# Linear attention in a four-layer kernel: denominators moved from TensorE matmuls to row sums on GpSimd and VectorE, with the order of keys, values and queries changed

## The chip, the cores and the metric

The kernel runs on one core of a Trainium2 chip. The metric is the device time of one execution in microseconds (us), as a median of several runs. The profile is one execution taken by the hardware profiler; its span is 1.75 to 2.93 us shorter than the time that is quoted for a run.

## The reference, cut to what matters

Four layers over 2048 tokens of width 1024: linear attention, feed-forward, linear attention, feed-forward, each with a layer norm in front and a residual sum behind. Only the attention layers are touched:

```
phi = lambda t: where(t > 0, t + 1, exp(t)) + 1e-6
pq, pk = phi(q), phi(k)                       # 32 heads of 32
kv  = einsum("bhsd,bhse->bhde", pk, v)
z   = pk summed over the tokens               # [head, d]
num = einsum("bhqd,bhde->bhqe", pq, kv)
den = einsum("bhqd,bhd->bhq", pq, z) + 1e-6   # one number per token and head
o   = (num / den) @ wo
```

Both kernels fold the output weight into kv (T = kv @ wo, once per layer), so the output is (pq / den) @ T.

## The kernel before

Queries are made feature-major (features in the partitions, 512 tokens in the columns). The sum z falls out of the key-value matmuls through a column of ones beside the values. The denominator is a matmul with z spread over each head's block; its reciprocal is exp(-ln(den)) on ScalarE.

```
def phi(self, ps, out):
    e = self.ep.tile([P, NW], F32, tag="e")
    nc.scalar.activation(out=e, in_=ps, func=ACT.Exp)
    nc.vector.tensor_scalar(out=e, in0=e, scalar1=1.0, scalar2=1e-6, op0=ALU.min, op1=ALU.add)
    nc.vector.scalar_tensor_tensor(out=out, in0=ps, scalar=0.0, in1=e, op0=ALU.max, op1=ALU.add)
...
def den(sc, g):                                # 32 per layer: 4 token groups x 8 feature tiles
    p = pq[sc, g // 4][:, g % 4, :]
    ps = self.ps3.tile([P, NW], F32, tag="b")
    nc.tensor.matmul(ps, lhsT=zrep[:, g, :], rhs=p, start=True, stop=True)
    r = self.ep.tile([P, NW], F32, tag="e")
    nc.scalar.activation(out=r, in_=ps, func=ACT.Ln, bias=self.eps6[:, 0:1])
    nc.scalar.activation(out=r, in_=r, func=ACT.Exp, scale=-1.0)
    nc.vector.tensor_tensor(out=p, in0=p, in1=r, op=ALU.mult)
...
later.at(4, finish_kv)
q_units(0, 5); fold_wo()                       # all 16 fold matmuls in one go
q_units(1, 2); out_units(0)
q_units(2, 2); out_units(1)                    # each q unit later makes one den
q_units(3, 2); out_units(2); out_units(3)
```

## Time and profile before

| | before |
|---|---|
| time, median | 1668.13 us |
| span in the profile | 1665.9 us |
| TensorE busy | 99% of the span |
| VectorE, ScalarE, GpSimd busy | 34%, 22%, 0% |
| denominator matmuls | 64 |

How to read it: a 512-column matmul has a record of 379 ns, but its successor starts after 216 ns. Busy time therefore says little. Time between two starts beyond the usual 216 ns is called a hole here; an eviction is the copy of a matmul's result out of PSUM, where this kernel's matmuls write. The lines that show the pace and the holes stand in the prediction.

### The profile page before, as it was taken

To read this page: it belongs to the slowest core of one execution; us is meant where nothing else is said; L and a number is where in the kernel's file an instruction comes from. 1 tells how busy PE (TensorE), PEld (TensorE's weight loads), DVE (VectorE), ACT (ScalarE), POOL (GpSimd) and SP (SyncE) were. 2 spreads that over 40 slices of the span, in tenths; PEclk is the share of its full clock that TensorE was granted. 3 is DMA by queue.
4 is the path that set the end of the run, shared out by engine and by line. 5 is a ranking of instruction groups with operands and counts; after the bars stand their busy time and mean duration, and the time that the engine had idled before them with its cause. 6 is when DMAs were issued, how large, how long until landed. Compare 5 with 4: busy or idle time off the path is not lost.

```text
span 1665.9 us, 18656 instructions
## 1 busy us (share of the span) xinstructions
PE 1644.1 (99%) x7678; PEld 751.3 (45%) x7834; DVE 571.6 (34%) x975; ACT 364.9 (22%) x695; POOL 4.8 (0%) x38
## 2 busy tenths in 40 slices
PE   8999999999999999999999999999999999999999
PEld 4444444444444444444444444444444444444444
DVE  7338994113221311311142398922111111111111
ACT  4337541100110110011033374411001101101110
POOL 0000000000000000000000000000000000000000
PEclk9999999999999999999999999999999999999999
DMA  9322134446445645644520312344554464455440
GB/s 297 57 64 89 32 95 127 142 145 171 153 138 186 177 142 158 170 154 138 174 75 1 94 58 45 95 121 144 186 169 149 142 190 147 144 178 164 149 153 28
DMA packets 262006, 218.28 MB, mean 131 GB/s; under 512 B 67232, under 2 KB 260000, under 8 KB 261920
## 3 DMA queue, kind: packets, MB, share of 16 engines
q1 hardware_dynamic: 257312, 212.88, 42.8%
q10 hardware_dynamic: 4608, 4.20, 0.7%
q8 instruction: 61, 1.00, 0.2%
q14 instruction: 25, 0.20, 0.0%
HBM read 197.13 MB, written 4.19 MB: 121 GB/s over the span
## 4 chain that ended last, share of the span: by engine, by line
PE 92%; DVE 4%; ACT 2%; issue 1%; DMA 1%; SPq 0%; another core or an unknown queue 0%
PE pg L433 23%; PE acc L450 23%; PE pu L433 23%; PE ps L295 13%; PE ps L364 4%; PE ps L377 4%; DVE stats L133 1%; PE kv L266 1%; DVE xn L149 1%; DVE x L384 1%; PE ps L335 1%; ACT r L337 1%; DMA x<-in_A_x_dram 1%; DVE pq L339 0%; ACT r L338 0%
## 5 line engine op out<-in xcount | busy, mean ns | idle before, releaser
L433 PEld LDWEIGHTS <-t 128*128 128x128 bf16 x3584 | 350.7, 98 | 422.9
L433 PE MATMUL pg<-xnT,t 128*128 128x512 bf16 x1757 | 420.2, 379 | 1.9
L433 PE MATMUL pu<-xnT,t 128*128 128x512 bf16 x1755 | 419.9, 379 | 1.9
L450 PE MATMUL acc<-t,hT 128*128 128x512 bf16 x1756 | 386.2, 379 | 1.9
L439 DVE TENSOR_TENSOR hT<-pu,rg 128x512 bf16<-128x512 f32 x224 | 154.9, 691 | 591.1 <-PE pu L433 568.7
L438 ACT ACTIVATE rg<-pg 128x512 f32<-128x512 f32 x224 | 133.6, 597 | 764.9 <-PE pg L433 690.3
L450 PEld LDWEIGHTS <-hT 128*128 128x128 bf16 x1792 | 175.4, 98 | 211.4
L295 PE MATMUL ps<-t,xnT 128*128 128x512 bf16 x999 | 224.3, 379 | 2.3 <-DVE xnT L201 0.8
L295 PEld LDWEIGHTS <-xnT 128*128 128x128 bf16 x1024 | 98.8, 98 | 115.3 <-DVE xnT L201 1.2
L364 PE MATMUL ps<-xnT,t 128*128 128x512 bf16 x500 | 119.8, 379 | 0.7
L377 PE MATMUL ps<-T,pq 128*128 128x512 bf16 x501 | 111.7, 379 | 0.6
L238 DVE TENSOR_SCALAR e<-e 128x512 f32<-128x512 f32 x128 | 54.3, 424 | 129.9 <-ACT e L237 129.0
L237 ACT ACTIVATE e<-ps 128x512 f32<-128x512 f32 x128 | 76.4, 597 | 91.5 <-PE ps L295 69.9
L140 ACT ACTIVATE rstd<-mv,eps 128x1 f32<-128x1 f32 x64 | 18.7, 294 | 306.9 <-DVE mv L138 306.6
L133 DVE BATCH_NORM_STATS2 stats<-x 128x6 f32<-128x512 f32 (+1 forms) x120 | 81.5, 685 | 2.0
L461 DVE TENSOR_TENSOR xo<-x,acc 128x512 bf16<-128x512 f32 x32 | 22.0, 688 | 171.8 <-PE acc L450 169.9
L377 PEld LDWEIGHTS <-pq 128*128 128x128 bf16 x512 | 50.1, 98 | 59.0
L364 PEld LDWEIGHTS <-t 128*128 128x128 bf16 x512 | 49.7, 98 | 55.0 <-issue 1.0
L458 DVE TENSOR_TENSOR x<-x,acc 128x512 f32<-128x512 f32 x32 | 21.6, 676 | 149.6 <-PE acc L450 148.4
L149 DVE TENSOR_SCALAR xn<-x,mv,rstd 128x1024 bf16<-128x1024 f32 (+2 forms) x65 | 47.8, 737 | 25.5 <-DMA xnT<-xn 18.3
L301 ACT ACTIVATE pkv<-ps 128x512 bf16<-128x512 f32 x64 | 38.1, 599 | 66.2 <-PE ps L295 64.4
L339 DVE TENSOR_TENSOR pq<-pq,r 128x512 bf16<-128x512 bf16 x64 | 43.6, 689 | 7.7 <-ACT r L338 5.6
(42 smaller groups left out, 377.8 us busy)
## 6 DMA issues: line engine op xcount, KB each, us to landing
t<-in_B_W_gate_dram SPq DMA_DIRECT2D x56, 1024.0 KB, 5.8
t<-in_B_W_up_dram SPq DMA_DIRECT2D x56, 1024.0 KB, 5.3
t<-in_B_W_down_dram SPq DMA_DIRECT2D x64, 896.0 KB, 5.7
t<-in_A_wqkv_dram SPq DMA_DIRECT2D x11, 1024.0 KB, 5.6
t<-in_A_wo_dram SPq DMA_DIRECT2D x4, 1024.0 KB, 5.3
out_dram<-xo ACTq DMA_DIRECT2D x32, 128.0 KB, 2.4
x<-in_A_x_dram SPq DMA_DIRECT2D x15, 256.0 KB, 7.8
t<-in_A_wqkv_dram SPq DMA_DIRECT2D x2, 512.0 KB, 5.1
```

The costliest lines, as they stand in the source:

```text
L133: self.nc.vector.bn_stats(out=stats[:, c, :], in_=src[:, c * fmax:(c + 1) * fmax])
L149: self.nc.vector.tensor_scalar(out=xn[:, s], in0=src[:, s], scalar1=mv[:, 0:1], scalar2=rstd[:, 0:1], op0=ALU.subtract, op1=ALU.mult)
L237: nc.scalar.activation(out=e, in_=ps, func=ACT.Exp)
L238: nc.vector.tensor_scalar(out=e, in0=e, scalar1=1.0, scalar2=1e-6, op0=ALU.min, op1=ALU.add)
L295: nc.tensor.matmul(ps, lhsT=self.xnT[l, q][:, kt, j * P:(j + 1) * P], rhs=w[:, kt, :], start=(kt == 0), stop=(kt == KT - 1))
L339: nc.vector.tensor_tensor(out=p, in0=p, in1=r, op=ALU.mult)
L364: nc.tensor.matmul(ps, lhsT=w[:, kt, (g % 4) * P:(g % 4 + 1) * P], rhs=self.xnT[l, sc][:, kt, :], start=(kt == 0), stop=(kt == KT - 1))
L377: nc.tensor.matmul(ps, lhsT=pq[sc, g // 4][:, g % 4, j * P:(j + 1) * P], rhs=T[g // 2][:, g % 2, n2 * NW:(n2 + 1) * NW], start=(g == 0), s ...
L433: nc.tensor.matmul(ps, lhsT=w[:, kt, fi * P:(fi + 1) * P], rhs=self.xnT[l, q][:, kt, :], start=(kt == 0), stop=(kt == KT - 1))
L438: nc.scalar.activation(out=rg, in_=pg, func=ACT.Relu)
L439: nc.vector.tensor_tensor(out=h[:, fi, :], in0=pu, in1=rg, op=ALU.mult)
L450: nc.tensor.matmul(acc[j], lhsT=hT[ft // 4][:, ft % 4, j * P:(j + 1) * P], rhs=wd[:, k, :], start=(ft == 0), stop=(ft == self.FT - 1))
```

## The change

The intent is to take the denominators off TensorE. Queries become token-major (128 tokens in the partitions), so that a denominator is the sum of 32 neighbouring columns of pq times z. GpSimd adds up the key features (`k_sum`), multiplies by z (`z_mult`) and scales (`z_scale`); VectorE sums rows and takes the reciprocal. The scaled queries are then transposed by DMA to serve as stationary operands (the ones that a weight load brings in: 512 loads of pqT in the changed kernel). So that GpSimd has time for it, all keys come before the values of the last two token groups, and queries alternate with these values, with the fold, and with the first outputs. Most of the query's phi moves from VectorE to ScalarE (three activations; one VectorE op stays). The weight ring shrinks from 7 tiles to 5, and two PSUM pools from 3 + 1 to 2 + 2.

The core of the diff, cut (the head's loads, pools and lists of units are left out):

```
-        def den(sc, g):
-            ... matmul with zrep, Ln, Exp(-), multiply ...
+        def k_sum(t):
+            if t == 0:
+                nc.gpsimd.tensor_copy(out=ksum, in_=pk[t])
+            else:
+                nc.gpsimd.tensor_tensor(out=ksum, in0=ksum, in1=pk[t], op=ALU.add)
+        def z_row():                           # round, sum over partitions and broadcast
+            nc.scalar.activation(out=hi, in_=ksum, func=ACT.Copy)
+            for i in range(H):
+                nc.tensor.matmul(ps, lhsT=self.ones, rhs=hi[:, i * NW:(i + 1) * NW], ...)
+                nc.scalar.activation(out=zrow[:, i * NW:(i + 1) * NW], in_=ps, func=ACT.Copy)
+        def q_unit(sc, j, c, lag):
+            nc.scalar.activation(out=e, in_=ps, func=ACT.Relu, scale=-1.0)
+            nc.scalar.activation(out=e, in_=e, func=ACT.Exp, scale=-1.0)
+            nc.scalar.activation(out=e, in_=e, func=ACT.Identity, bias=self.eps6[:, 0:1])
+            nc.vector.scalar_tensor_tensor(out=pq[...], in0=ps, scalar=0.0, in1=e, max, add)
+        def z_mult(pq, sc, j):
+            nc.gpsimd.tensor_tensor(out=prod, in0=pq, in1=zrow, op=ALU.mult)
+        def z_sum(pq, prod, sc, j):
+            nc.vector.tensor_reduce(out=den, in_=heads(prod), axis=X, op=ALU.add)
+            nc.vector.tensor_scalar(out=den, in0=den, scalar1=1e-6, scalar2=None, op0=ALU.add)
+            nc.vector.reciprocal(out=den, in_=den)
+        def z_scale(pq, den, sc, j):
+            nc.gpsimd.tensor_tensor(out=heads(pq), in0=heads(pq), in1=den broadcast, op=ALU.mult)
+            nc.sync.dma_start_transpose(out=pqT[sc][:, :, j * P:(j + 1) * P], in_=pq)
...
+        # values and keys of groups 0 and 1, keys of 2 and 3, then:
+            later.at(4, z_row)
+            run(q_of(0, 4), v_then_kv(2))
+            run(q_of(1, 1), v_then_kv(3))
+            later.at(2, finish_kv)
+            run(q2[:5])
+            run([with_fold(u, i) for i, u in enumerate(q2[5:] + q3[:5])])   # 2 folds per unit
+            run(q3[5:], out0[:3])
```

## The prediction

The sum came to 1643.5 + 2 x (0.3 + 1 + 2 + 1) = 1652 us. Of its terms, the 0.3 (key blocks) and the first 1 (broadcast of the key sums) stand as guesses of mine, worked out from no trace. So do the 1660 to 1668 of the last rival. The floor and the 2 and 1 us at the fold come from the trace of the kernel before, with the choices that the text names. Its "about 0.73 with bias" is an estimate that fits that trace: 0.636 us for an activation without bias (L338) plus the 0.690 - 0.597 between L337 with one and L237 without. The one pace is seen in the chain of waits, where 49 matmuls take 10.74 us on L295, L377 and L450 alike.

> **What bounds the kernel now.** I read the page's busy line first, then the chain of waits, then the groups of instructions with their shapes kept apart, then the timeline of TensorE where the chain leaves it.
>
> ```profile
> PE 1644.1 (99%) x7678; PEld 751.3 (45%) x7834; DVE 571.6 (34%) x975; ACT 364.9 (22%) x695; POOL 4.8 (0%) x38
> PE 92%; DVE 4%; ACT 2%; issue 1%; DMA 1%; SPq 0%; another core or an unknown queue 0%
> ```
>
> TensorE is busy 99% of the span and is 92% of the chain that ended last; no other engine passes 34%. The kernel is a matmul stream with small holes. The real pace is read from the chain in order of time, near its end:
>
> ```profile
> 1618.94 10.74 PE acc L450 x49
> 1629.73 10.74 PE acc L450 x49
> 1640.52 10.74 PE acc L450 x49
> ```
>
> The pieces start 10.79 us apart. Each shows 49 matmuls of a period of 50 (a record goes missing now and then, which the count of weight loads confirms: 1792 loads against 1756 matmuls on that line). So one 512-column matmul costs 10.79/50 = **0.2158 us**, although its record says 379 ns[...]. The pace is one constant for all stages.
>
> I add up by weight loads: the feed-forward layers have 3584 + 1792 = 5376, which is 1160.2 us. The attention layers have 1024 (keys and values) + 512 (queries) + 512 (outputs) = 2048, which is 442.0 us; 64 denominators, 13.8 us; 32 for folding the output weight, 6.9 us. The 256 key-value products start 8 in 0.48 us (40.35 to 40.83 in the timeline), 0.06 each, 15.4 us. Sum 1638.3 of a span of 1665.9. The other 27.6 us: by 19.59 us only 33 projections (7.1 us) had been started, so the head costs 12.5; the last matmul ends at 1662.5, so the tail costs 3.4. The remaining **11.7 us** are holes, and some small transposes, inside the attention layers. The timeline and the waits of TensorE show the holes:
>
> ```profile
> 145.52 3.57 PE L349 MATMUL ps<-t,kvT 128*128 128x512 bf16 x12
> 149.29 0.38 PE L349 MATMUL ps<-t,kvT 128*128 128x512 bf16 x1 [0.20 <-ACT T L352]
> ...
> 181.47 4.48 PE L364 MATMUL ps<-xnT,t 128*128 128x512 bf16 x20
> 186.76 0.39 PE L335 MATMUL ps<-pq,zrep 128*128 128x512 bf16 x1 [0.82 <-DVE pq L239]
> ```
>
> Denominator matmuls (L335) stop the stream until VectorE has made the query features; the fold (L349) runs ahead of its evictions: 12 matmuls take 3.57 us where the pace gives 2.6.
>
> [...]
>
> **The change part by part.** The groups it removes are these:
>
> ```profile
> L335 PE MATMUL ps<-pq,zrep 128*128 128x512 bf16 x64 | 23.9, 384 | 4.2 <-DVE pq L239 3.9
> L337 ACT ACTIVATE r<-ps,eps 128x512 f32<-128x512 f32 x64 | 43.4, 690 | 9.5 <-PE ps L335 9.2
> L338 ACT ACTIVATE r<-r 128x512 f32<-128x512 f32 x64 | 39.9, 636 | 1.5
> L339 DVE TENSOR_TENSOR pq<-pq,r 128x512 bf16<-128x512 bf16 x64 | 43.6, 689 | 7.7 <-ACT r L338 5.6
> ```
>
> Only the first lies on the path: 64 x 0.2158 = 13.8 us, not the 23.9 of its busy time. Added on TensorE are 4 matmuls that broadcast the key sums (0.9 us); the 16 small transposes of the key-value matrix become a DMA transpose. If every hole also closed, the gain would be 13.8 + 11.7 - 0.9 = **24.6 us**: a floor of 1668.1 - 24.6 = 1643.5. Nothing else shortens the stream: projections, outputs, fold and feed-forward keep their counts, head and tail their order. A gain over 2% needs 1634.8, out of reach by this sum.
>
> What comes back, per attention layer:
> - Keys. GpSimd adds 16 key tiles[...] in bursts of four (one per 1.73 us unit, in the second half of each block)[...]. I put 0.3 us.
> - Key sums. [...] ScalarE rounds it (kvT's 1024 columns took 1.02 us). The broadcast stands in TensorE's order after four units, 6.9 us. TensorE waits some 1 us.
> - Queries beside values. Per token tile TensorE has 6.9 us. ScalarE: two queries of three activations (0.60 + 0.64 + about 0.73 with bias) and two values (0.60), 5.1[...]. No loss.
> - Fold among queries. The build order puts the first fold after five query units: 5 x 1.73 + 0.5 = 9.1 us. Its input needs the last key-value product (2.2 us), the masking behind the second query's eviction on VectorE (about 7.9), then a DMA transpose; the layer-norm ones landed in a median 3.1 us, up to 9.9 behind weights. So 11 to 13 us: a wait of 2 us or a bit more. From there a unit is 1.73 + 2 x 0.216 = 2.16 us for TensorE, against ScalarE 1.97 + 0.60 = 2.57[...]. Eight units: ScalarE falls 3.3 us behind; buffers and the wait just paid hide most. I put 1 us.
> Sum 0.3 + 1 + 2 + 1 = 4.3 us, twice 8.6. **1643.5 + 8.6 = 1652 us.** Where I chose: the lag that buffers hide (I let them hide two thirds) and the 2 us wait.
>
> The weight ring shrinks from 7 to 5 tiles. In the feed-forward a pair is used in 32 matmuls x 2 = 13.8 us and loaded in 5.8 + 5.3 us; the second of a pair is issued at the start of the pair before and needed 15.5 us later. It fits, so I give it nothing.
>
> **The rivals.**
> - GpSimd becomes the bound. If an op on bf16 with a broadcast operand took 4 us, the 16 last query ops in the pure-query stretch (8 tiles x 8 us = 64 against 40) would stop the stream some 20 us per layer, since VectorE's reduction waits in order for the product and there is one product buffer. Time about 1690 to 1705.[...]
> - The ring starves the feed-forward. If each of 56 pairs waited 0.5 us, +28: 1680. For it: the DMA share is 0.5 there, and transposes share the queue; against: 11.1 of 15.5 us.
> - All hidden: the buffers absorb everything, 1644.
> - The gain vanishes[...]: 1660 to 1668.
>
> **Range and chances.** The low end is the floor, 1643.5, rounded to 1643. The high end, 1664, takes about 10 us back per layer. Faster by over 2% contradicts the matmul count: 0.02. Slower by over 2% (1701) needs slow GpSimd ops or a starving ring: 0.04. Within 2%: 0.94.
>
> **What would show it.** Right: no denominator matmuls, weight loads down by 76 (64 + 16 removed, 4 added), the same 0.2158 pace, feed-forward stages of the same length to 1 us[...], and TensorE's waits at the fold on the DMA of kvT and at the key-sum broadcast on ScalarE. Wrong: GpSimd rows over 3 us, TensorE waiting on evictions all through the key blocks, or weight loads that TensorE waits for in the feed-forward.

## The result

The changed kernel takes **1648.28 us** (1647.47 to 1649.50, 4 runs), against 1667.81 us for the kernel before in the same rounds: 19.5 us less. The ratio is 0.9884, with an interval from 0.9866 to 0.9901. A ratio is the mean time of one kernel's runs over that of the other's of the same rounds, so it is not quite the ratio of the medians.

The busy line, the chain by engine, and three groups of the changed kernel:

```profile
PE 1634.7 (99%) x7758; PEld 747.5 (45%) x7758; DVE 575.1 (35%) x930; ACT 372.2 (23%) x699; POOL 196.5 (12%) x102
...
PE 91%; DVE 3%; ACT 2%; POOL 1%; issue 0%; DMA 0%; DVEq 0%; POOLq 0%
...
L356 POOL TENSOR_TENSOR prod<-pq,zrow 128x1024 f32<-128x1024 bf16 x32 | 68.1, 2128 | 53.4 <-DVE den L361 35.5
...
L299 POOL TENSOR_TENSOR ksum<-ksum,pkv 128x1024 f32<-128x1024 f32 x30 | 65.5, 2182 | 68.9 <-DVE pkv L245 67.7
...
L367 POOL TENSOR_TENSOR pq<-pq,den 128x1024 bf16<-128x1024 bf16 x32 | 61.2, 1911 | 17.9 <-issue 10.6
```

The stream still bounds the kernel; weight loads fell from 7834 to 7758, and GpSimd went from nothing to 196.5 us. What TensorE itself waited for, from the waits of TensorE in the changed kernel (total us, times, longest; the wait before the warm-up is left out):

```profile
PE tp L203 <- DVE xn L152: 2.1, 1, 2.1
PE ps L322 <- ACT hi L319: 1.5, 2, 0.7
PE ps L284 <- DMA t<-in_A_wqkv_dram: 0.9, 1, 0.9
PE ps L284 <- DVE xnT L206: 0.8, 2, 0.5
PE ps L377 <- DMA kvT<-kvm: 0.6, 2, 0.3
PE kv L311 <- DVE pkv L245: 0.6, 1, 0.6
```

The second line is the broadcast of the key sums, the fifth the fold's wait for the transposed key-value matrix, the last a key-value product in the first layer. The others are in the head. Such a wait counts from the modelled end of the matmul before, so it is shorter than the real hole. The real hole is the time between two matmul starts less the usual 0.216 us: 0.9 us per layer at the broadcast (1.121 between starts), 0.51 and 0.44 at the first fold, 0.73 at the key-value product.

With the time of each matmul counted from its start to the next one's start, the trace gives a full account (a missing record's time falls to the matmul before it):

| TensorE, us | before | after |
|---|---|---|
| warm-up and transposes in the head | 7.7 | 6.8 |
| projections of keys, values, queries | 339.5 | 341.0 |
| key-value products | 16.0 | 15.0 |
| transposes of the key-value matrix | 0.9 | 0 |
| denominators, or broadcast of z | 15.5 | 0.9 |
| fold | 9.8 | 7.1 |
| outputs | 110.7 | 110.5 |
| feed-forward layers | 1160.1 | 1160.1 |
| sum | 1660.2 | 1641.4 |

The difference is 18.8 us; the two spans differ by 18.7. The feed-forward is the same to a tenth of a microsecond, so the shorter ring and the smaller PSUM pool cost nothing there. The projections took 331.5 us at the pace in both kernels, so their holes are 8.0 us before and 9.5 after. The row of the key-value products needs care: four missing records of projections put 0.86 us into the 16.0, and the 15.0 contains the hole of 0.73. The runs without denominators below have neither; there they take 15.1 and 14.3 us (59 ns from start to start with 129 columns, 56 with 128). Of the 9.5 us of holes, 4.6 are in the head of this one execution (2.8 before), a matter that the second profile of the same kernel below sets apart.

### The profile page after: what moved, and what is told of

Its sections match the earlier page's. It is cut to its first block, busy times and chain, and to the rows that moved or that the text cites. A ratio compares the mean times of both kernels' runs of the same rounds, so it can differ in the third digit from the quotient of the medians.

```text
span 1647.2 us, 18687 instructions
## 1 busy us (share of the span) xinstructions
PE 1634.7 (99%) x7758; PEld 747.5 (45%) x7758; DVE 575.1 (35%) x930; ACT 372.2 (23%) x699; POOL 196.5 (12%) x102
## 4 chain that ended last, share of the span: by engine, by line
PE 91%; DVE 3%; ACT 2%; POOL 1%; issue 0%; DMA 0%; DVEq 0%; POOLq 0%
PE acc L523 23%; PE pu L506 23%; PE pg L506 23%; PE ps L284 13%; PE ps L389 7%; POOL ksum L299 1%; DVE e L244 1%; PE kv L311 1%; DVE pkv L245 1%; ACT e L347 0%; ACT e L346 0%; ACT T L381 0%; ACT e L348 0%; DVE pq L349 0%; DVE den L361 0%
## 5 line engine op out<-in xcount | busy, mean ns | idle before, releaser
L506 PEld LDWEIGHTS <-t 128*128 128x128 bf16 x3584 | 350.7, 98 | 422.8
L284 PE MATMUL ps<-t,xnT 128*128 128x512 bf16 x1536 | 344.7, 380 | 1.7 <-DMA t<-in_A_wqkv_dram 0.9
L284 PEld LDWEIGHTS <-xnT 128*128 128x128 bf16 x1536 | 149.0, 98 | 177.7 <-issue 5.6
L389 PE MATMUL ps<-T,pqT 128*128 128x512 bf16 x512 | 111.5, 379 | 0.0
L143 ACT ACTIVATE rstd<-mv,eps 128x1 f32<-128x1 f32 x64 | 18.8, 294 | 335.4 <-DVE mv L141 335.4
L389 PEld LDWEIGHTS <-pqT 128*128 128x128 bf16 x512 | 50.1, 98 | 60.4
L356 POOL TENSOR_TENSOR prod<-pq,zrow 128x1024 f32<-128x1024 bf16 x32 | 68.1, 2128 | 53.4 <-DVE den L361 35.5
L299 POOL TENSOR_TENSOR ksum<-ksum,pkv 128x1024 f32<-128x1024 f32 x30 | 65.5, 2182 | 68.9 <-DVE pkv L245 67.7
L349 DVE SCALAR_TENSOR_TENSOR pq<-ps,e 128x512 bf16<-128x512 f32 x64 | 43.4, 679 | 82.0 <-ACT e L348 81.7
L244 DVE TENSOR_SCALAR e<-e 128x512 f32<-128x512 f32 x64 | 52.7, 823 | 48.9 <-ACT e L243 48.5
L367 POOL TENSOR_TENSOR pq<-pq,den 128x1024 bf16<-128x1024 bf16 x32 | 61.2, 1911 | 17.9 <-issue 10.6
L243 ACT ACTIVATE e<-ps 128x512 f32<-128x512 f32 x64 | 38.1, 596 | 70.9 <-PE ps L284 69.6
```

The source lines that it names most:

```text
L284: nc.tensor.matmul(ps, lhsT=self.xnT[l, l_q][:, kt, j * P:(j + 1) * P], rhs=w[:, kt, :], start=(kt == 0), stop=(kt == KT - 1))
L299: nc.gpsimd.tensor_tensor(out=ksum, in0=ksum, in1=pk[t], op=ALU.add)
L349: nc.vector.scalar_tensor_tensor(out=pq[:, c * NW:(c + 1) * NW], in0=ps, scalar=0.0, in1=e, op0=ALU.max, op1=ALU.add)
L356: nc.gpsimd.tensor_tensor(out=prod, in0=pq, in1=zrow, op=ALU.mult)
L367: nc.gpsimd.tensor_tensor(out=heads(pq), in0=heads(pq), in1=den[:, :].unsqueeze(2).to_broadcast([P, D // HD, HD]), op=ALU.mult)
L389: nc.tensor.matmul(ps, lhsT=pqT[sc][:, g, j * P:(j + 1) * P], rhs=T[g // 2][:, g % 2, n2 * NW:(n2 + 1) * NW], start=(g == 0), stop=(g == G ...
```

## The experiments

**1. Where the gain comes from: both kernels without denominators.** The rival to my account was that the new order made the gain. Both runs give wrong results on purpose.

Before without denominators:

```
-                later.at(lag, lambda g=g: den(sc, g))
```

> Before with its denominators left out (wrong result on purpose; their matmuls, activations and multiplications go, everything else stays). Theory: the matmuls (64 x 0.2158 = 13.8 us) and the holes at them (about 6.8 us in the gaps between matmul starts) are the gain, so 1667.8 - 20.6 = 1647, perhaps 1 less since the fold's evictions meet an idler ScalarE. Rival: the gain of the change came from the new order of the parts; then this run stays over 1653.

Measured: **1644.96 us** (1644.16 to 1646.24); before 1667.88. That is 22.9 us less, 2.3 us more than the 20.6 of the theory. Most of the difference is the fold, whose 32 matmuls fell from 9.8 to 8.2 us now that no ln and exp stand among its evictions.

The change without denominators (key sums, broadcast, product, row sum, reciprocal and scaling left out, the DMA transposes kept):

```
-                later.at(1, lambda: k_sum(t))
-            later.at(4, z_row)
-                later.at(lag, lambda: z_mult(pq, sc, j))
+                later.at(lag + 4, lambda: z_scale(pq, None, sc, j))     # only the transpose is left
```

> The changed kernel with its denominators left out (wrong result on purpose: no key sums, no broadcast, no product, row sum, reciprocal or scaling). Theory: what denominators still cost there is the broadcast (4 matmuls, 0.9 us), the wait in front of it (0.9 us per layer) and the hole in the first key block (0.6 us), so 1648.3 - 3.3 = 1645.0; the fold's holes stay, since ScalarE makes them. Rival: GpSimd and VectorE work makes the fold's holes too; then 1643 or less. Against the run of before without denominators: if both are within 3 us of each other, the order of the parts alone is worth little.

Measured: **1645.47 us** (1644.87 to 1646.04). Both kernels without denominators are within 0.5 us, so the rest of the change, the order included, is worth nothing on balance. The denominators cost 22.9 us in the old form and 2.8 us in the new one; the difference is the gain. The rival has fallen. The balance hides two sides, though: the trace of this run saves the transposes of the key-value matrix (0.9 us) and 0.8 us of key-value products, and pays 4.1 us of holes at the fold, where the kernel before without denominators has 1.3 us of holes in its attention layers. With no product, row sum or scaling left, these holes cannot come from them.

**2. What the new form still costs: collisions between VectorE and GpSimd.** In the key blocks the min-and-add of phi is the same instruction in both kernels. First line: the kernel before (all uses of phi), from its source view, with durations min/median/max in ns; second fence: the changed kernel (keys only).

```profile
L238 DVE TENSOR_SCALAR e<-e x128: 408/427/428, 29.1 to 1054.8; 128x512 f32<-128x512 f32 x128
```

```profile
L244 DVE TENSOR_SCALAR e<-e x64: 375/427/2359, 31.1 to 916.3; 128x512 f32<-128x512 f32 x64
```

The median stays at 427 ns, but the maximum goes from 428 to 2359, and the mean to 823 (its group's 52.7 us over 64). The trace shows it one by one: 22 of the 64 records are longer than 0.6 us, and 21 of these start during a key sum on GpSimd and end 0.28 to 0.29 us after that sum. Such an op is called blocked here; the blocked time stands inside its own record. The chain of waits of the changed kernel at the end of the keys, in order of time (start, length), shows what it leads to:

```profile
88.00 1.56 DVE e L244
...
90.27 1.55 DVE e L244
...
98.42 2.18 POOL ksum L299
...
105.22 2.13 POOL ksum L299
...
107.37 1.06 ACT hi L319
...
108.48 0.59 PE ps L322 x2
```

An op that takes 0.42 us when free takes 1.5 to 2 us here, VectorE falls behind, the last four key sums run back to back from 98.42 to 107.35, and the rounded sums reach TensorE 0.9 us late. But is it the collision, or merely GpSimd's own 2.2 us per tile? To take the collision away, phi of the keys was made without the min-and-add ("that op" in the expectation):

```
-            self.phi(project(f"k{c}", q, j), pk[t][:, c * NW:(c + 1) * NW])
+            ps = project(f"k{c}", q, j)
+            e = self.ep.tile([P, NW], F32, tag="e")
+            nc.scalar.activation(out=e, in_=ps, func=ACT.Relu, scale=-1.0)
+            nc.scalar.activation(out=e, in_=e, func=ACT.Exp, scale=-1.0)
+            nc.vector.scalar_tensor_tensor(out=pk[t][...], in0=ps, scalar=1e-6, in1=e, max, add)
```

> The changed kernel with phi of the keys made by two activations (relu of -x, exp of the negative) and one VectorE op[...]; the result stays right. Theory (collisions of that op with GpSimd delay the key sums): GpSimd's last burst ends in time, the wait before the broadcast (0.9 us per layer) and the hole of 0.6 us in the first key block go, 1648.3 - 2.4 = 1646. Rival: GpSimd's own 2.2 us per tile delays it; then the wait stays and the time is 1648.

Measured: **1646.40 us** (1645.59 to 1647.78), correct. The wait for the rounded sums is no longer among TensorE's waits (the hole is 0.15 us), nor is the one of the key-value product. The last four sums still take 8.8 us (8.9 in the changed kernel), but they start 2.85 us before the first query matmul, not 2.25, and are ready 5.9 us after it, not 6.7. These 0.76 us are what the wait lost. So GpSimd's own speed makes most of the delay, and the collisions make the part that TensorE waited for. The edit also takes VectorE's own work away (64 x 0.427 = 27.3 us, beside the 25.4 us of blocked time), and this run cannot part the two; but 0.43 and 0.69 us of work per unit of 1.73 us would not put VectorE behind.

The hole at the first layer's key-value product had another source. The op in front of the late key is a layer-norm scaling (L152) that starts during a key sum and is recorded with 2.35 us, against a median of 0.81. From the chain of the changed kernel:

```profile
43.92 2.27 DVE xn L152
46.19 0.61 DVE pkv L245
46.80 0.05 issue
46.85 0.40 PE kv L311 x4
```

It is still blocked in this run (2.11 us), where the hole is gone, and in the combined version of section 5 the hole is back (0.58 us). So that this edit closed it is not shown.

The same wait can be avoided by order alone:

```
-            later.at(4, z_row)
+            later.at(6, z_row)
```

> The changed kernel with the broadcast of the key sums two units (3.45 us) later in TensorE's order, nothing else. Theory: TensorE's wait of 0.9 us per layer for the rounded key sums was a matter of order alone, and GpSimd, which idles before its first product anyway, does not mind: 1648.3 - 1.8 = 1646.5. Rival: a later start of the products pushes GpSimd's work into the stretch around the fold and gives the gain back there: 1648.

Measured: **1646.34 us** (1646.22 to 1646.71). The hole at the broadcast is 0.24 us per layer, the waits at the fold are as they were, so the products did not push GpSimd's work into the fold. Its theory holds.

**3. The holes at the fold: ScalarE or VectorE.** Windows of the changed kernel around the fold (start:end, length, then busy us of PE, weight loads, VectorE, ScalarE, GpSimd with the number of instructions, then granted clock, DMA share and GB/s):

```profile
160.00:194.00 34.00, 33.39 (x158) 14.79 (x157) 25.98 (x44) 30.65 (x53) 26.62 (x14) 1.00 0.53 124
```

ScalarE has 30.65 of 34 us, the most beside TensorE. The gaps between matmul starts at the fold, beyond the first, are 1.1 us in the first attention layer and 1.2 in the third layer. The third activation of a query only adds 1e-6; it can go into the max:

```
-            nc.scalar.activation(out=e, in_=e, func=ACT.Identity, bias=self.eps6[:, 0:1])
-            nc.vector.scalar_tensor_tensor(out=pq[...], in0=ps, scalar=0.0, ...
+            nc.vector.scalar_tensor_tensor(out=pq[...], in0=ps, scalar=1e-6, ...
```

> The changed kernel with two activations per query unit in place of three (the 1e-6 goes into the max of the VectorE op, a difference far under bf16). Theory: ScalarE, busy 30.65 of 34 us around the fold, makes the holes at the fold (about 1.1 us per layer beyond the wait for the DMA transpose); they go, 1648.3 - 2.2 = 1646. Rival: VectorE's row sums and evictions make them; then under 0.5 us is gained.

Measured: **1645.29 us** (1645.01 to 1646.79), correct: 3.0 us less, not the 2.2 expected, and far over the rival's 0.5. By the trace the holes at the fold fell from 3.25 to 0.58 us, both layers together. The same window in this run:

```profile
160.00:194.00 34.00, 34.00 (x164) 15.51 (x163) 27.60 (x48) 23.00 (x39) 28.02 (x15) 1.00 0.59 143
```

ScalarE is down to 23.00, and TensorE shows no idle time in the window. The wait for the transposed matrix went too, although its DMA takes about as long (3.0 us after 3.1): it was issued 7.4 us after the queries' start, not 8.1, since the masking in front of it stands behind a query's eviction on VectorE, and that waits for ScalarE.

Next, that wait attacked by order: the fold one query unit later.

```
-            run(q2[:5])
-            run([with_fold(u, i) for i, u in enumerate(q2[5:] + q3[:5])])
-            run(q3[5:], out0[:3])
-            run(out0[3:])
+            run(q2[:6])
+            run([with_fold(u, i) for i, u in enumerate(q2[6:] + q3[:6])])
+            run(q3[6:], out0[:2])
+            run(out0[2:])
```

> The changed kernel with the fold starting one query unit (1.73 us) later, beside six units of the last query tile group instead of five. Theory: the wait for the DMA transpose (0.5 us per layer) goes and ScalarE's lag meets the same evictions one unit later, so the other fold holes stay: 1648.3 - 0.95 = 1647.3. Rival: with the wait gone ScalarE has that much less time to catch up, and the fold's holes grow by the same amount: 1648.3.

Measured: **1649.46 us** (1649.01 to 1650.59): worse by 1.2 in the median. The runs overlap with those of the change (up to 1649.50), but the trace has 0.9 us more of holes at the fold. The DMA wait did go, but TensorE's waits now have this:

```profile
PE ps L377 <- DVE T L383: 1.7, 2, 0.8
```

A fold matmul waits for an eviction that now stands behind a row sum on VectorE (1.0 us between starts beyond the pace, in both layers), and ScalarE's holes are still there. My theory fell, and it went even further than the rival: not only is nothing gained, a new wait came.

**4. How much room GpSimd has.** Each product is done twice:

```
             nc.gpsimd.tensor_tensor(out=prod, in0=pq, in1=zrow, op=ALU.mult)
+            nc.gpsimd.tensor_tensor(out=prod, in0=pq, in1=zrow, op=ALU.mult)
```

> The changed kernel with each GpSimd product of query features and key sums done twice (same result). Theory: GpSimd is near its limit around the fold, busy 26.6 of 34 us; 7 more products of 2.13 us there are 41.5 of 34, and VectorE's row sums wait in order for them, so TensorE loses 5 to 8 us per layer: 1658 to 1664. Rival: buffers hide GpSimd's lag; then under 1652. GpSimd busy should read 196.5 + 68 = 265 us.

Measured: **1684.06 us** (1683.69 to 1684.85), slower than before (ratio 1.0098). GpSimd reads 263.9 us busy, as expected; TensorE lost 35.8 us, 17.9 per layer, where I had 5 to 8. From the waits of this run, all engines:

```profile
DVE den L362 <- POOL prod L357: 68.2, 24, 5.2
...
PE ps L378 <- DVE T L384: 10.7, 7, 2.6
PE ps L390 <- DVE x L397: 10.6, 6, 2.5
...
PE ps L284 <- DVE pq L349: 6.0, 3, 2.9
```

VectorE's row sums waited 68.2 us for products (3.9 in the changed kernel), and everything behind them in VectorE's order waited too: fold evictions, query evictions, and the residual sums of the outputs. I had counted the loss only up to the end of the fold and had forgotten that the lag is carried into the outputs: 6.6 us of holes per layer are there. Up to the end of the fold the loss is still some 11 us per layer, so the 5 to 8 were too few there too. The direction is shown: one more 2.13 us op per token tile is more than the schedule holds.

**5. A version that beats both.** First all helpful edits and the later fold together (broadcast one unit later, at 5):

> The version that should beat both: keys' phi with two activations and one VectorE op, two activations per query, the broadcast one unit later, the fold one unit later. Theory: the gains of the single edits add, since each takes away another hole: broadcast 1.8, first key block 0.6, fold 2.2, wait for the transposed key-value matrix 0.95: 1648.3 - 5.6 = 1642.7, within 1 us of the floor of 1643.5 that was computed before. Rival: the holes hide behind each other, so the sum is no more than the best single edit, 1645.

Measured: **1644.22 us** (1644.15 to 1644.78), correct, 1.5 over the theory: the sum of the single gains was not reached. Its waits have a fold eviction on VectorE again (`PE ps L381 <- DVE T L387`, 0.8 us in all), which fits the loss in the run with the later fold alone; the hole at the first key-value product is there too. So the fold went back:

> The version with all three edits that helped (keys' phi with two activations and one VectorE op, two activations per query, broadcast one unit later) but the fold where the change has it. Theory: what held the version with the fold one unit later at 1644.2 was that its fold's eviction stood behind a row sum on VectorE (holes of 0.58 us per layer); with the fold back they go: 1644.2 - 1.2 = 1643.0. Rival: with the earlier fold the wait for the transposed key-value matrix comes back; then 1644 or more.

Measured: **1643.71 us** (1642.54 to 1644.52), correct, ratio to before 0.9852 (0.9836 to 0.9869). The waits of TensorE have no line of the attention layers any more. Its four runs overlap those of the version before it, so the last 0.5 us are shown by the profile, not by the times: the holes at the fold fell from 1.3 to 0.6 us, both layers together. Another 0.5 us between the two profiles is the hole at the first key-value product, which no edit between them touches. The holes in the attention layers add up to about 0.8 us in the trace.

> The changed kernel as it is, on the same chip as the best version. Theory: 1648.3 again, 5 us above the best version; TensorE waits for the rounded key sums in both layers. The half-rate matmuls in the head may or may not come, since only some profiles have them.

Measured: **1648.06 us** (1647.89 to 1649.18), 4.4 above the best version on the same chip. The span of this profile is 1645.7 us, 1.5 less than the first one's, with the same holes in the attention layers to 0.2 us each; the difference is the head. There the first profile has a gap of 2.07 us and behind it six matmuls at 427 ns from start to start, twice the usual. This one has none. So 1.5 us of the first profile's 9.5 us of holes are not the change's.

## Why the prediction was right

The prediction said 1652 (1643 to 1664), within 2%; measured were 1648.28 and 1648.06. It was right, and mostly for its reasons.

- **The bound and the pace.** Right. Weight loads fell by 76, the feed-forward stayed, and the account by starts adds up to the difference of the spans. One reading is rough: 12 fold matmuls up to the end of the last record are 11 x 0.2158 + 0.379 = 2.75 us at the pace, not 2.6.
- **The gross gain of 24.6 us.** Right within the noise. The floor of 1643.5 is what the best version reached (1643.71). Leaving out the denominators gave 22.9, and 1.3 us of holes were left in that run, 1.0 of them before fold matmuls. The only term that was missing is the key-value products, 0.8 us cheaper with 128 columns than with 129.
- **GpSimd's cost.** Measured were 2.18, 2.13 and 1.91 us (key sums in a burst start 2.25 to 2.28 us apart), 196.5 us in all.
- **Given back: 8.6 us predicted; the holes measured in the first profile add up to 5.8.** Term by term, for both layers together:

| hole | predicted | measured |
|---|---|---|
| key blocks | 0.6 | 0.7, in one layer |
| broadcast of the key sums | 2 | 1.8 |
| wait for the transposed matrix | 4 | 0.95 |
| other holes at the fold | 2 | 2.3 |

The term that was off is the wait for the transposed matrix, "2 us or a bit more" per layer, and the step of it that failed is "the build order puts the first fold after five query units: 5 x 1.73 + 0.5 = 9.1 us". The first fold stands behind a sixth unit, which is in the same list item as the fold itself, so it is due after 6 x 1.73 + 0.45 = 10.8 us. The timeline of TensorE in the changed kernel shows it (start, length, instruction):

```profile
158.66 3.62 PE L284 MATMUL ps<-t,xnT 128*128 128x512 bf16 x16
162.11 0.61 PE L311 MATMUL kv<-pkv 128*128 128x128 bf16 x8
162.56 8.80 PE L284 MATMUL ps<-t,xnT 128*128 128x512 bf16 x40
171.70 0.60 PE L377 MATMUL ps<-t,kvT 128*128 128x512 bf16 x2 [0.35 <-DMA kvT<-kvm]
```

The first line is the last value unit and the first unit of the queries, which therefore starts at 162.11 - 1.73 = 160.4; the third line is five more query units. The other times of that step were right: the masking ended and the DMA was issued at 168.54, 8.1 us after the queries' start (7.9 predicted), and took 3.12 us, so the matrix was there after 11.3 (11 to 13 predicted). Against 10.8 that leaves the measured half microsecond. The sum 1643.5 - 0.8 + 5.8 = 1648.5 comes near the measured 1648.28.

- **Cause of the fold's holes.** I put them on ScalarE; the run with two activations shows it.
- **Cause of the broadcast's wait.** Collisions, but not as I had them, and the right 1 us is partly luck: I had put the collisions into the length of the burst of sums, a guess. The burst started 2.25 us before the keys end and lasted 8.9, so ready after 6.7. VectorE's op was blocked (1.5 to 2 us) and GpSimd's sums in the burst were not stretched (2.13 to 2.21 us): the collisions delayed the start.
- **Key blocks.** The number was a guess and is right by luck. Not every min-and-add collided with a key sum (21 of 64), and the one hole stands behind the blocked layer-norm op, which the prediction did not have.
- **The rivals.** The starving ring did not happen: no wait for weights in the feed-forward. "All hidden" did not happen either, but the best version comes near it. GpSimd as the bound did not happen, yet it is close: the run with double products is what that rival described.

What stays open: why the head's wait for a first weight tile is 0.9 us in one profile and absent in others of the same load order.

## What to carry to other kernels

Count the matmuls of a stream that bounds a kernel at their start-to-start pace (0.216 us here, beside a record of 379 ns). Here work taken off the stream was worth that pace and the waits in front of it (22.9 us measured, 20.6 by that count), and the order alone was worth nothing on balance (1644.96 and 1645.47 us without denominators). Work given to GpSimd was cheap here, 2.8 us for all denominators, but two things took time from the stream: key sums that blocked VectorE's ops, in front of the 0.9 us per layer at the broadcast (0.15 in the run without the min-and-add), and row sums that waited in VectorE's order for GpSimd's products, behind the 35.8 us of the run with double products. The first is seen in the maximum (2359 ns), not the median (427), of a VectorE group, the second in VectorE's waits (68.2 us against 3.9). Where a wait remains, look which engine is fullest in that window: taking one activation from ScalarE there, 30.65 of 34 us busy, cut the holes at the fold from 3.25 to 0.58 us, and moving the fold in the order made a new one of 1.0 us per layer. Moving the broadcast did help: its hole fell from 0.9 to 0.24 us per layer.

## Further figures from the traces

- The time for which a key sum on GpSimd blocks a VectorE op stands inside the blocked op's record: 2359 ns at most for the min-and-add, against a median of 427.
- For 1024 columns GpSimd took 2.13 us for bf16 times bf16 to fp32, 2.18 for fp32 plus bf16, 1.91 for bf16 times a broadcast fp32 operand to bf16, and 1.14 for a cast, all in the changed kernel.
- In the head of the changed kernel a gap of 2.07 us (matmul starts 2.45 us apart), with smaller ones in the microseconds before it, was followed by six matmuls at 427 ns instead of 216; the granted clock from 12 to 19 us was 0.76, and 1.00 in the second profile of the same kernel. The length of one gap does not decide alone: in that second profile starts 2.12 us apart were not followed by any, and in the run with two activations per query starts 1.97 us apart were followed by at least three.
- On VectorE a reciprocal of 32 columns took 0.353 us and a row sum of 1024 columns 1.21 us.
